# Attention, a dense block and a routed block on one core: three slot tables, and the experts' weights split half an expert ahead

## The chip, the cores and the metric

The kernel runs on one core of one Trainium2 chip. The metric is the device time of one execution in microseconds (us). A core has five engines that run their own instruction queues in order: PE (matrix multiply; its weight loads are listed as PEld), DVE (vector), ACT (scalar), POOL and SP. In this kernel SP issues the plain transfers and POOL the gathers and scatters by index.

## The reference, cut to what matters

```
attn = softmax(mask_64(q k^T / 8)) v               # 4 x 576 tokens = 2304, 8 heads of 64
x    = prelu(attn @ w_in, alpha) @ w_out            # 512 -> 2048 -> 512
logits = x @ w_gate                                 # 8 experts
e    = argmax(logits); p = softmax(logits)[e]
out  = p * (relu(x @ w1[e]) @ w2[e])                # 512 -> 1024 -> 512, only the chosen expert
```

All arrays are float32. The kernel gets that precision by splitting each operand into a high part (rounded to the matmul's format, float32r) and a low part (the rest), and adding three products: high by high, high by low, low by high.

## The kernel before

The 2304 tokens are 18 tiles of 128. They go through attention and the dense block in five blocks of 4, 4, 4, 3 and 3 tiles. `PLAN`, a list of short tokens, gives the order of all work up to the last block. For block j and hidden chunk f (16 of them), `s1` is the first matmul (12 instructions), `act_neg`, `act_sum`, `g_hi`, `g_lo` are the activation and the split, and `s2` the second matmul (9 instructions for 3 tiles).

Behind each block comes the routing of its tokens. `stage_out` copies x out of PSUM; the logits are dot products on DVE (`r_row` loads a row of the gate's weights, `r_dot` multiplies), and for the last block matmuls on PE (`r_trans`, `r_logits`); `r_gate` finds the expert and writes x with its factor to DRAM (`x1d`); `r_rank`, `r_place`, `r_onehot`, `r_list` and `r_add` enter each token into a list by expert.

The experts' stage works in slots: a slot is up to 128 tokens of one expert. `slot_table` says which expert and which piece of its list each slot takes. There are 25 slots, of which the given input uses 21; the first 20 run always, the others under a condition. The first table (6 slots) is made when four blocks are routed and takes full tiles only; the second (19 slots) is made when all are routed and takes the rest.

A slot s runs so: `gather` picks its 128 token numbers on DVE and fetches the rows by a transfer that POOL issues. `xtr` transposes them on PE, copies the high part on ACT and subtracts the low part on DVE. `e1` is the first matmul, in four quarters of 6 instructions; relu on ACT after two of them; `htr` transposes and splits the hidden half; `e2mm` is the second matmul, four quarters of 6; `finish` scales on ACT and scatters. The order on PE is

```
e1 q0, e1 q1, e1 q2, transpose half 0, e1 q3, e2 q0, transpose half 1, e2 q1, transpose x of s+1, e2 q2, e2 q3
```

The expert's weights are 4 MB in four transfers to `raw2[0..3]` (a transfer is skipped if the expert stays the same). They are split in eight pieces, a copy on ACT (`split2_hi`, 128x1024) and a subtraction on DVE (`split2_lo`) each, into 12 ring tiles: the eight of slot s, and four more. A split is made in every slot, whether the expert changes or not. In `slot(s)`, step i splits piece i of slot s+1 and, at each second step, asks for a transfer for slot s+2. The last block is written as a loop with `fill` for what goes between (routing of the fourth block, first table, weights of the first slot), ordered by the framework's scheduler; the slots follow by hand order (`manual_schedule`). The routing of the last block and the second table lie in slots 0 to 3 (`extra`).

Of the kernel before, what the change touches and what calls it, by code (L numbers as in the profile page):

```python
# [19 lines left out]
K1 = 6  # L20
SURE = 20
LO_POOL = ()
# [4 lines left out]
NBT = 4  # L27
PE_MASK = 4
# [52 lines left out]
def attn_moe_moe_kernel(  # L81
# [55 lines left out]
    wgc = const.tile([128, 4, 2 * NE], FP32R, name="wgc")  # L137
# [392 lines left out]
    def r_place(j):  # L530
# [9 lines left out]
        give(("R", j))  # L540
# [19 lines left out]
    def r_onehot(j, h=0):  # L560
        t0, n = BLOCKS[j]
        cf, pf = rc[j]
        ab[j] = []
        for t in range(2 * h, min(2 * h + 2, n)):
# [5 lines left out]
            ab[j].append((t, a, bm))  # L570
# [18 lines left out]
    fill = {}  # L589

    def at(it, prio, fn, *a):
        fill.setdefault(it, []).append((prio, fn, a))

    def run_fill(it):
        for _, fn, a in sorted(fill.pop(it, []), key=lambda e: e[0]):
            fn(*a)

# [3 lines left out]
    def slot_table(part):  # L601
        ns, s0 = (K1, 0) if part == 0 else (NSLOT - K1, K1)

        def small(nm, shape, dt=FP32):
            n = {"cmp": ns * NE, "es": ns, "jn": ns}.get(nm)
            pad = {} if n is None else {"padded_shape": [128, NSLOT] if len(shape) == 1 else [128, NSLOT, NE]}
# [10 lines left out]
        give(("R", NB))  # L617
        yield
# [6 lines left out]
        yield  # L625
# [5 lines left out]
        yield  # L631
# [16 lines left out]
        yield  # L648
# [8 lines left out]
        else:  # L657
            done = small("done", [NE])
# [9 lines left out]
    def table_step():  # L668
        next(gen1, None)
# [381 lines left out]
```

## Time and profile before

| what | value |
|---|---|
| median of 3 runs | 768.34 us (767.71 to 769.11) |
| the profiled execution | 768.02 us |
| its span on the core | 766.2 us |
| PE busy | 747.7 us (98%) |
| DVE busy | 609.1 us (79%) |
| ACT busy | 456.3 us (60%) |
| POOL busy | 89.0 us (12%) |

The last block begins near 415 us, the first slot near 486 us, and the last slot's matmuls end near 758.5 us. A busy time is the time in which an engine had an instruction running; matmuls overlap one another, so PE's busy time hides short waits. The queue before each engine is in order: an instruction that waits holds all behind it.

### The profile page before, as it was taken

How to read it: one execution, taken by the hardware profiler on the slowest of the kernel's cores; microseconds unless marked ns; L12 is line 12 of the kernel's file. 1: busy time of each engine (PE TensorE's matmuls, PEld its weight loads, DVE VectorE, ACT ScalarE, POOL GpSimd, SP SyncE). 2: the span in 40 equal slices, each digit the busy share in tenths (PEclk: the TensorE clock that was granted, in tenths of full speed). 3: DMA queues.
4: the chain of work that ended last, by engine and by line, in shares of the span. 5: the costliest groups of instructions: out<-in, count | busy, mean ns of one | idle time of the engine just before them, and what ended most of it. 6: DMA issues, size and time to landing. Idle time of an engine off the chain costs nothing.

```text
span 766.2 us, 12642 instructions
## 1 busy us (share of the span) xinstructions
PE 747.7 (98%) x4567; PEld 612.6 (80%) x4572; DVE 609.1 (79%) x1154; ACT 456.3 (60%) x868; POOL 89.0 (12%) x106
## 2 busy tenths in 40 slices
PE   7999999999999999999999999999999999999996
PEld 3688888788888888888888988777788888888884
DVE  4999999477556656668775956699999999999997
ACT  4887465533233333334342323778889898899986
POOL 1210001000000000000000001011222213131322
PEclk9999999999999999999999999999999999999998
DMA  9993423233033113122323116430195076766621
GB/s 343 412 367 131 147 74 117 70 86 122 18 100 97 62 57 103 62 97 90 92 69 111 56 42 250 168 119 28 56 340 182 29 270 265 284 236 248 212 75 51
DMA packets 29442, 109.90 MB, mean 143 GB/s; under 512 B 3582, under 2 KB 3966, under 8 KB 22208
## 3 DMA queue, kind: packets, MB, share of 16 engines
q1 hardware_dynamic: 25856, 98.25, 35.6%
q0 software_dynamic: 3520, 10.80, 4.2%
q8 instruction: 38, 0.62, 0.3%
q14 instruction: 28, 0.23, 0.1%
HBM read 154.09 MB, written 10.26 MB: 214 GB/s over the span
## 4 chain that ended last, share of the span: by engine, by line
PE 86%; DVE 8%; issue 2%; DMA 1%; ACT 1%; POOL 0%; SPq 0%; DVEq 0%
PE acc L743 12%; PE h L389 9%; PE acc L431 9%; PE acc L432 9%; PE h L390 8%; PE h L391 8%; PE acc L433 8%; DVE hl L825 4%; PE h L715 4%; PE h L717 4%; PE h L716 4%; PE att L364 2%; PE att L295 2%; PE att L341 2%; PE att L726 1%
## 5 line engine op out<-in xcount | busy, mean ns | idle before, releaser
L825 DVE TENSOR_TENSOR hl<-hl,hl 128x1024 fp32r<-128x1024 f32 x176 | 211.4, 1223 | 17.1 <-ACT hl L819 16.4
L819 ACT CAST hl<-hl 128x1024 fp32r<-128x1024 f32 x176 | 180.2, 1049 | 4.6 <-DMA hl<-in_wx_dram 3.4
L743 PE MATMUL acc<-hl,xl 128*128 128x512 f32 x504 | 130.7, 400 | 2.4 <-DVE xl L730 2.3
L404 ACT ACTIVATE g<-h 128x512 f32<-128x512 f32 (+1 forms) x80 | 44.6, 557 | 142.6 <-PE h L391 112.3
L389 PE MATMUL h<-xh,hl 128*128 128x512 f32 (+1 forms) x320 | 120.5, 377 | 0.7 <-DVE g L408 0.7
L390 PE MATMUL h<-xl,hl 128*128 128x512 f32 (+1 forms) x320 | 118.1, 369 | 0.0
L391 PE MATMUL h<-xh,hl 128*128 128x512 f32 (+1 forms) x320 | 118.0, 369 | 0.0
L432 PE MATMUL acc<-hl,gl 128*128 128x512 f32 x288 | 113.2, 393 | 0.4 <-DVE gl L414 0.4
L433 PE MATMUL acc<-hl,gh 128*128 128x512 f32 x288 | 112.6, 391 | 0.0
L431 PE MATMUL acc<-hl,gh 128*128 128x512 f32 x288 | 109.9, 400 | 0.0
L743 PEld LDWEIGHTS acc<-hl,xl 128*128 128x128 f32 x504 | 91.2, 188 | 21.3 <-DVE xl L730 3.7
L408 DVE SCALAR_TENSOR_TENSOR g<-g,beta,h 128x512 f32<-128x512 f32 (+1 forms) x80 | 55.3, 691 | 56.1 <-ACT g L404 55.9
L414 DVE TENSOR_TENSOR gl<-g,gh 128x512 fp32r<-128x512 f32 (+1 forms) x80 | 50.8, 635 | 38.4 <-PE acc L432 24.1
L349 ACT CAST gh<-g 128x512 fp32r<-128x512 f32 (+1 forms) x80 | 46.5, 581 | 51.4 <-DVE g L408 49.7
L691 POOL DMA_INDIRECT gx<-x1d,ixg x23 | 39.9, 1736 | 290.5 <-DVE xh L703 167.1
L389 PEld LDWEIGHTS h<-xh,hl 128*128 128x128 f32 x320 | 60.1, 188 | 10.9 <-issue 1.2
L715 PE MATMUL h<-hl,xh 128*128 128x512 f32 x168 | 67.7, 403 | 0.0
L485 DVE SCALAR_TENSOR_TENSOR dot<-stage,wge 128x512 bf16<-128x512 f32 x96 | 65.9, 686 | 1.8 <-DMA wge<-in_wgt_dram 0.4
L390 PEld LDWEIGHTS h<-xl,hl 128*128 128x128 f32 x320 | 60.1, 188 | 8.5 <-DVE xl L377 0.5
L717 PE MATMUL h<-hl,xh 128*128 128x512 f32 x168 | 66.1, 393 | 0.3 <-DVE xh L703 0.2
L391 PEld LDWEIGHTS h<-xh,hl 128*128 128x128 f32 x320 | 60.1, 188 | 7.9
L716 PE MATMUL h<-hl,xh 128*128 128x512 f32 x168 | 65.5, 390 | 0.0
(194 smaller groups left out, 1070.8 us busy)
## 6 DMA issues: line engine op xcount, KB each, us to landing
hl<-in_wx_dram SPq DMA_DIRECT2D x92, 1024.0 KB
hl<-in_wcat_dram SPq DMA_DIRECT2D x14, 1024.0 KB
qk<-in_qkv_dram SPq DMA_DIRECT2D x30, 448.0 KB
v<-in_qkv_dram SPq DMA_DIRECT2D x30, 256.0 KB
wge<-in_wgt_dram SPq DMA_DIRECT2D x24, 256.0 KB
x1d<-stage SPq DMA_DIRECT2D x3, 1032.0 KB
hl<-in_qkv_dram SPq DMA_DIRECT2D x6, 448.0 KB
x<-in_wcat_dram SPq DMA_DIRECT2D x2, 1024.0 KB
```

The costliest lines, as they stand in the source:

```text
L389: PE.matmul(out=h[:, 0:n], lhsT=w_in_op(f, k, 0), rhs=xh[:, k, :], start=(k == 0), stop=False)
L390: PE.matmul(out=h[:, 0:n], lhsT=w_in_op(f, k, 0), rhs=xl[:, k, :], start=False, stop=False)
L391: PE.matmul(out=h[:, 0:n], lhsT=w_in_op(f, k, 1), rhs=xh[:, k, :], start=False, stop=(k == 3))
L431: PE.matmul(out=a, lhsT=gh[:, c0:c0 + 128], rhs=w_out_op(f, 0), start=(f == 0), stop=False)
L432: PE.matmul(out=a, lhsT=gl[:, c0:c0 + 128], rhs=w_out_op(f, 0), start=False, stop=False)
L433: PE.matmul(out=a, lhsT=gh[:, c0:c0 + 128], rhs=w_out_op(f, 1), start=False, stop=(f == 15))
L715: PE.matmul(out=o, lhsT=th[:, k, :], rhs=wh, start=(k == 0), stop=False)
L716: PE.matmul(out=o, lhsT=th[:, k, :], rhs=wl, start=False, stop=False)
L717: PE.matmul(out=o, lhsT=tl[:, k, :], rhs=wh, start=False, stop=(k == 3))
L743: PE.matmul(out=o, lhsT=x[:, f % 4, :], rhs=w[:, lo, (f % 2) * 512:(f % 2) * 512 + 512], start=(x is th and f == 0 and lo == 0), stop=(x i ...
L819: ACT.copy(out=t[:, 0, :], in_=r)
L825: eng.tensor_tensor(out=t[:, 1, :], in0=r, in1=f32(t[:, 0, :]), op=ALU.subtract)
```

## The change

`PARTS` makes three tables, of 5, 3 and 17 slots, after three, four and five blocks. The loop of the last block, `fill` and `extra` go; a second list, `PLAN2`, gives the order from the last block's start to the end of slot 8, with one token for each piece of work: `s R t h l u` the dense block (64 to 79 is the last block's f 0 to 15), `N D Z G J j M I i` routing by dot products, `rt ra rl rc` the last block's logits, `y` a step of a table, `v w` the SP register loads and weight transfers, `a d` the two halves of a split (8 for each slot), `g gp` pick and fetch, `Q A f` the three parts of `xtr`, `E k F U z K` a slot's matmul quarters, relu, transposes and their split, `o op` scale and scatter. From slot 9 on, `slot` is the hand order below: it splits pieces 4 to 7 of slot s+1 in its first half and pieces 0 to 3 of slot s+2 in its second. The ring tiles come in the order in which the dense block frees them. The last block's logits are plain float32 matmuls on x as it is, without a split; the split copy of the gate's weights goes, and two float32 filler matmuls near 25 us become four bfloat16 ones. Each transpose takes one of three PSUM banks from a list of free ones.

```diff
-K1 = 6
+PARTS = [(0, 5), (5, 3), (8, 17)]
 SURE = 20
+NPLAN = 9
...
+Q0 g1 R74 J3 a1 u73 t74 gp1 j3 h74 s75 g2 l74 gp2 M6 y3 u74 R75 a3 t75 y4 h75 a5 s76 A0 l75 d1 Q1 R76 u75 A1 t76 w4
...
+w27 F10 E23 gp7 U10 z10 v8 I9 k11 d50 F11 K20 d51 U11 a52 i9 K21 w29 z11 a55 d53 K22 a54 d52 K23 a56 d55 w30 v9 a57
+E24 d56 a59 d54 E25 a58 d57 w31 E26 k12 i8 w32 y8 a60 F12 E27 U12 d58 Q7 z12 k13 A7 d59 F13 K24 U13 d60 a61 w33 K25
+E31 U14 d66 a69 Q8 z14 w37 k15 v11 d68 a71 F15 K28 d69 U15 A8 K29 o6 z15 w38 a70 op6 d71 K30 a72 f8 d70 a73 K31 d72
+a74 w39 E32 a75 d73 E33 a76 d75 w40 E34 k16 d74 a77 F16 d76 w41 a78 E35 d77 U16 k17 z16 a79 w42 F17 g9 K32 d78 o7
+U17 op7 K33 z17 a80 d79 gp9 K34 a81 d80 w43 K35 a82 d81 g10 o8 w44 d82 a83 gp10 d83 op8 w45 Q9 A9 f9
...
     def r_logits(j, t):
-        th, tl = x1t.pop((j, t))
-        n = BLOCKS[j][1]
-        b = rbank(j)
+        x = x1t.pop(t)
+        b = aslot(("rl", t))
+        w = wg.rearrange("p (k e) -> p k e", k=4)
         for k in range(4):
-            PE.matmul(out=b[:, 0:2 * NE], lhsT=th[:, k, :], rhs=wgc[:, k, :], start=(k == 0), stop=False)
-            PE.matmul(out=b[:, 0:NE], lhsT=tl[:, k, :], rhs=wgc[:, k, 0:NE], start=False, stop=(k == 3))
-        lo = rp.tile([128, NE], FP32, tag="lo", name="lo")
-        ACT.copy(out=lo, in_=b[:, NE:2 * NE])
-        DVE.tensor_tensor(out=rt[j][:, t, :], in0=b[:, 0:NE], in1=lo, op=ALU.add)
...
+            PE.matmul(out=b[:, 0:NE], lhsT=x[:, k, :], rhs=w[:, k, :], start=(k == 0), stop=(k == 3))
...
     def ring_tile(s, i):
-        p = 4 + (8 * s + i) % 12
+        p = W_AT[4 + (8 * s + i) % 12]
...
+        toks = [f"E{4 * s}", *both(n, 4), f"E{4 * s + 1}", f"k{2 * s}", *both(n, 5), f"w{4 * s + 10}" if r2 else "",
+                f"E{4 * s + 2}", f"F{2 * s}", f"U{2 * s}", f"z{2 * s}", *both(n, 6), f"E{4 * s + 3}", f"k{2 * s + 1}",
+                *both(n, 7), f"w{4 * s + 11}" if r2 else "", f"K{4 * s}", f"F{2 * s + 1}", f"U{2 * s + 1}",
+                f"z{2 * s + 1}", *both(n + 1, 0)]
+        toks += [f"g{s + 2}", f"gp{s + 2}"] if r2 else []
+        toks += [f"K{4 * s + 1}"] + ([f"Q{n}", f"A{n}", f"f{n}"] if n < NSLOT else []) + both(n + 1, 1)
+        toks += [f"v{s + 3}", f"w{4 * s + 12}"] if r3 else []
+        toks += [f"K{4 * s + 2}", *both(n + 1, 2), f"K{4 * s + 3}", f"o{s}", f"op{s}", *both(n + 1, 3),
+                 f"w{4 * s + 13}" if r3 else ""]
...
-        for s in range(SURE):
+        for o in PLAN2.split():
+            play(o)
+        for s in range(NPLAN, SURE):
             slot(s)
```

How this moves instructions shows in three places. First DVE in slot 4 of before: L825 is a split's subtraction, L730 the low part of a transposed hidden half, L650 to L656 the end of the second table.

```order
L654 TENSOR_TENSOR cmp<-cmp,done 128x152
L655 TENSOR_REDUCE jn<-cmp 128x19
L656 TENSOR_TENSOR col<-col,jn 128x19
L825 TENSOR_TENSOR hl_4809<-hl_4700,hl_4809 128x1024
L825 TENSOR_TENSOR hl_4841<-hl_4700,hl_4841 128x1024
L825 TENSOR_TENSOR hl_4927<-hl_4694,hl_4927 128x1024
L825 TENSOR_TENSOR hl_4933<-hl_4694,hl_4933 128x1024
L730 TENSOR_TENSOR xl<-acc_4983,xl 128x512
```

DVE in slot 4 of the changed kernel: L840 is a split's subtraction, L728 the low part of a hidden half (`xl`) or of x (`xh`), L579 and L581 the last block's one-hot tiles.

```order
L728 TENSOR_TENSOR xl<-att_68,xl 128x512
L840 TENSOR_TENSOR hl_5050<-hl_4511,hl_5050 128x1024
L840 TENSOR_TENSOR hl_5068<-hl_4627,hl_5068 128x1024
L728 TENSOR_TENSOR xl<-att_68,xl 128x512
L840 TENSOR_TENSOR hl_5032<-hl_4627,hl_5032 128x1024
L840 TENSOR_TENSOR hl_4679<-hl_4432,hl_4679 128x1024
L579 TENSOR_SCALAR A<-c,cf 128x152
L581 TENSOR_SCALAR B<-c,pf 128x128
```

Behind a table's steps four splits stood ahead of the hidden half in before; now two stand between one half and the next.

Second, PE at the end of slot 4 of before (L717 the last of `e1` q3, L743 a quarter of `e2`, L726 the transposes of hidden half 1, L699 those of the next slot's x):

```order
L717 MATMUL h<-hl_5063,xh 128x512
L743 MATMUL acc_5067<-hl_4745,xl 128x512 x6
L726 MATMUL att_67<-c,hr 128x128 x4
L743 MATMUL acc_5067<-hl_4777,xl 128x512 x6
L699 MATMUL att_68<-c,gx 128x128 x4
L743 MATMUL acc_5067<-hl_4809,xl 128x512 x6
L743 MATMUL acc_5067<-hl_4841,xl 128x512 x6
L715 MATMUL h<-hl_4927,xh 128x512
```

and PE at the end of slot 8 of the changed kernel, the last of `PLAN2` (L747 the last of `E35`, L717 with `hr` is `F17`, L763 are `K32` to `K35`, L717 with `gx` is `Q9`, then slot 9 begins):

```order
L747 MATMUL h<-hl_5014,xh 128x512
L717 MATMUL acc_4255<-c,hr 128x128 x4
L763 MATMUL acc_5156<-hl_5032,xl 128x512 x6
L763 MATMUL acc_5156<-hl_5068,xl 128x512 x6
L763 MATMUL acc_5156<-hl_5125,xl 128x512 x6
L763 MATMUL acc_5156<-hl_5153,xl 128x512 x6
L717 MATMUL att_67<-c,gx 128x128 x4
L745 MATMUL h<-hl_4679,xh 128x512
```

The transposes of hidden half 1 stand right behind the quarter that makes it, no longer behind a quarter of `e2`; those of slot 9's x stand right ahead of slot 9.

Third, the same place on ACT (L835 `a82`, L768 `o8`, L835 `a83`, L722 `A9`) and on DVE (`g10`, `d82`, `d83`, `f9`) in the changed kernel:

```order
L835 CAST hl_5125<-hl_4511 128x1024
L768 ACTIVATE gx<-acc_5156,gx 128x512
L835 CAST hl_5153<-hl_4511 128x1024
L722 CAST xh<-att_67 128x512
L835 CAST hl_4679<-hl_4627 128x1024
```

```order
L704 CAST ixs<-ixf 128x1
L840 TENSOR_TENSOR hl_5125<-hl_4511,hl_5125 128x1024
L840 TENSOR_TENSOR hl_5153<-hl_4511,hl_5153 128x1024
L728 TENSOR_TENSOR xh<-att_67,xh 128x512
L840 TENSOR_TENSOR hl_4679<-hl_4627,hl_4679 128x1024
```

The low part of slot 9's x (`f9`) stands behind the last split of `PLAN2` (`d83`), whose copy (`a83`) stands behind the scaling of slot 8 (`o8`) and writes the ring tile that `K35` reads.

## Rows read from the trace of the kernel before

**Rows 1.** The page: span, and busy time of each engine.
```profile
span 766.2 us, 12642 instructions
...
PE 747.7 (98%) x4567; PEld 612.6 (80%) x4572; DVE 609.1 (79%) x1154; ACT 456.3 (60%) x868; POOL 89.0 (12%) x106
```

**Rows 2.** Timeline of ACT: scaling of slots 0, 4 and 20 (start, duration).
```profile
506.39 0.69 ACT L749 ACTIVATE gx<-acc,gx 128x512 f32<-128x512 f32 x1 [0.26 <-PE acc L743]
...
561.79 0.69 ACT L749 ACTIVATE gx<-acc,gx 128x512 f32<-128x512 f32 x1 [0.27 <-PE acc L743]
...
758.80 0.69 ACT L749 ACTIVATE gx<-acc,gx 128x512 f32<-128x512 f32 x1 [0.29 <-PE acc L743]
```

**Rows 3.** Busy us by stretch: length, PE, PEld, DVE, ACT, POOL; clock, DMA, GB/s.
```profile
430.00:470.00 40.00, 40.00 (x209) 35.76 (x208) 26.84 (x105) 9.68 (x20) 1.80 (x2) 1.00 0.19 63
470.00:490.00 20.00, 18.93 (x89) 15.31 (x88) 13.80 (x17) 11.16 (x17) 0.32 (x1) 1.00 0.70 290
...
510.00:560.00 50.00, 46.67 (x224) 36.56 (x223) 48.88 (x95) 40.23 (x53) 8.82 (x6) 1.00 0.22 72
...
680.00:700.00 20.00, 20.00 (x99) 16.55 (x98) 19.17 (x26) 17.82 (x24) 5.82 (x4) 1.00 0.51 171
```

**Rows 4.** Timeline of DVE and PE in slot 4.
```profile
550.68 4.67 DVE L825 TENSOR_TENSOR hl<-hl,hl 128x1024 fp32r<-128x1024 f32 x4
...
554.09 1.09 PE L743 MATMUL acc<-hl,xl 128*128 128x512 f32 x4
...
555.27 0.68 DVE L730 TENSOR_TENSOR xl<-acc,xl 128x512 fp32r<-128x512 f32 x1
...
556.00 0.73 PE L743 MATMUL acc<-hl,xl 128*128 128x512 f32 x2 [0.82 <-DVE xl L730]
```

**Rows 5.** Timeline of PE: end of the last block, logits of the last block.
```profile
470.04 0.34 PE L389 MATMUL h<-xh,hl 128*128 128x384 f32 x1
...
472.15 0.86 PE L431 MATMUL acc<-hl,gh 128*128 128x512 f32 x3
...
481.58 0.86 PE L431 MATMUL acc<-hl,gh 128*128 128x512 f32 x3
...
483.66 0.60 PE L699 MATMUL att<-c,gx 128*128 128x128 f32 x4
484.01 0.95 PE L431 MATMUL acc<-hl,gh 128*128 128x512 f32 x3
...
494.89 0.26 PE L463 MATMUL att<-wgc,xh 128*128 128x16 f32 x1
...
495.79 0.47 PE L715 MATMUL h<-hl,xh 128*128 128x512 f32 x1
```

**Rows 6.** Groups by line: instructions, busy us, mean ns of one, idle before.
```profile
L825 DVE TENSOR_TENSOR hl<-hl,hl 128x1024 fp32r<-128x1024 f32 x176 | 211.4, 1223 | 17.1 <-ACT hl L819 16.4
L819 ACT CAST hl<-hl 128x1024 fp32r<-128x1024 f32 x176 | 180.2, 1049 | 4.6 <-DMA hl<-in_wx_dram 3.4 <-PE acc L433 1.2
...
L720 ACT ACTIVATE hr<-h 128x512 f32<-128x512 f32 x42 | 25.2, 600 | 6.3 <-PE h L717 6.2
...
L703 DVE TENSOR_TENSOR xh<-att,xh 128x512 fp32r<-128x512 f32 x22 | 15.0, 681 | 0.0
L749 ACT ACTIVATE gx<-acc,gx 128x512 f32<-128x512 f32 x21 | 14.5, 690 | 5.7 <-PE acc L743 5.7
```

**Rows 7.** Timeline of PE and ACT in slot 20: last matmul of a half, its relu.
```profile
748.75 0.39 PE L717 MATMUL h<-hl,xh 128*128 128x512 f32 x1
...
749.24 0.60 ACT L720 ACTIVATE hr<-h 128x512 f32<-128x512 f32 x1 [0.20 <-PE h L717]
```

**Rows 8.** Timeline of PE near 25 us: the two float32 filler matmuls.
```profile
25.06 1.46 PE L275 MATMUL att<-c 128*128 128x384 f32 x4
```

**Rows 9.** Timeline at the end: the last splits, the last transfer issued.
```profile
759.23 2.50 DVE L825 TENSOR_TENSOR hl<-hl,hl 128x1024 fp32r<-128x1024 f32 x2
...
761.75 0.07 SPq L764 DMA_DIRECT2D hl<-in_wx_dram  x1
```

More of the change, by code (lines that the diff above doesn't have):

```diff
@@ L575, in r_list, with r_add @@
     def r_list(j, h=0):
-        lbs[j] = rbank(j)
-        some = ab.pop(j)
+        lbs[j, h] = aslot(("I", j, h))
+        some = ab.pop((j, h))
         for i, (t, a, bm) in enumerate(some):
-            PE.matmul(out=lbs[j][:, 0:NCOL], lhsT=bm, rhs=a, start=(i == 0), stop=(i == len(some) - 1))
+            PE.matmul(out=lbs[j, h][:, 0:NCOL], lhsT=bm, rhs=a, start=(i == 0), stop=(i == len(some) - 1))
     lbs = {}
-    def r_add(j):
-        DVE.tensor_tensor(out=lst, in0=lst, in1=lbs.pop(j)[:, 0:NCOL], op=ALU.add)
-        give(("R", j))
+    def r_add(j, h):
+        DVE.tensor_tensor(out=lst, in0=lst, in1=lbs.pop((j, h))[:, 0:NCOL], op=ALU.add)
+        give(("I", j, h))
     NB = len(BLOCKS)
[L589 to L596, printed above, removed]
     tab = {}
@@ L657, in slot_table, with table_step @@
         else:
+            tab["scr"] = small("scr", [NCOL])
+        if not final:
             done = small("done", [NE])
             DVE.tensor_tensor(out=done, in0=nb, in1=cum, op=ALU.subtract)
-            DVE.tensor_scalar(out=done, in0=done, scalar1=float(K1), scalar2=0.0, op0=ALU.add, op1=ALU.max)
+            DVE.tensor_scalar(out=done, in0=done, scalar1=float(ns), scalar2=0.0, op0=ALU.add, op1=ALU.max)
             DVE.tensor_tensor(out=done, in0=done, in1=nb, op=ALU.min)
+            if part:
+                DVE.tensor_tensor(out=done, in0=done, in1=tab["done"], op=ALU.add)
             tab["done"] = done
             tab["last"] = ec[:, ns - 1:ns]
-            tab["scr"] = small("scr", [NCOL])
         tab["col", part] = col
         yield
-    def table_step():
-        next(gen1, None)
+    gens = {}
+    def table_step(part):
+        if part not in gens:
+            gens[part] = slot_table(part)
+        next(gens[part])
     def where(s):
-        return (0, s) if s < K1 else (1, s - K1)
+        p = max(i for i, (s0, _) in enumerate(PARTS) if s >= s0)
+        return p, s - PARTS[p][0]
     gat = {}
@@ L679, in attn_moe_moe_kernel, with rows, pick @@
     ops = {}
-    def gather(s):
+    def rows(s):
+        j = NB - len(PARTS) + 1 + where(s)[0]
+        return NT if j == NB else BLOCKS[j][0] * 128
+    def pick(s):
         ixf = rot("ixf", 2, [128, 2], FP32)
@@ L717, in e1, with relu @@
             PE.matmul(out=o, lhsT=tl[:, k, :], rhs=wh, start=False, stop=(k == 3))
-        if kk == 1:
-            hr[s, a] = rot("hr", 2, [128, 512], FP32)
-            ACT.activation(out=hr[s, a], in_=hps.pop((s, a)), func=ACTF.Relu)
-    def htr(s, a):
-        x = hr.pop((s, a))
-        b = pbank("att").rearrange("p (k c) -> p k c", k=4)
-        for k in range(4):
-            PE.transpose(b[:, k, :], x[:, k * 128:k * 128 + 128], ident)
-        th = rot("hth", 2, [128, 4, 128], FP32R)
-        tl = rot("htl", 2, [128, 4, 128], FP32R)
-        ACT.copy(out=th, in_=b)
-        DVE.tensor_tensor(out=tl, in0=b, in1=f32(th), op=ALU.subtract)
-        hT[s, a] = (th, tl)
+    def relu(s, a):
+        hr[s, a] = rot("hr", 2, [128, 512], FP32)
+        ACT.activation(out=hr[s, a], in_=hps.pop((s, a)), func=ACTF.Relu)
     def e2mm(s, ff):
@@ L958, in attn_moe_moe_kernel, with both @@
-    gen1 = slot_table(1)
+    st1.close()
+    e2 = ctx.enter_context(tc.tile_pool(name="e2", bufs=2, reuse_waits="tile"))
+    late = True
+    attb.append(bank("acc3", 1))
+    idle.append(2)
+    def slot(s):
+        def both(n, i):
+            i += 8 * n
+            return [f"a{i}", f"d{i}"] if n < NSLOT else []
+        n = s + 1
+        r2, r3 = s + 2 < NSLOT, s + 3 < NSLOT
+        toks = [f"E{4 * s}", *both(n, 4), f"E{4 * s + 1}", f"k{2 * s}", *both(n, 5), f"w{4 * s + 10}" if r2 else "",
[7 more added lines that the diff above has]
+                 f"w{4 * s + 13}" if r3 else ""]
+        for o in toks:
+            if o:
+                play(o)
```

270 lines of the change are left out of this document (107 added, 163 removed).

## The prediction

> **What bounds the kernel now.** I read the page first: PE is busy 747.7 of a span of 766.2 us, DVE 609.1 and ACT 456.3 [rows 1]. The profiled execution took 768.02 us, 1.8 around its span; the median of the runs shown is 0.32 above it. A gain can thus only come from PE's waits, from fewer PE instructions, or from the ends. Next came the windows of each stretch [rows 3]. The clock granted to PE is 1.00 (the 2.4 GHz level) in all four, so no time is to be had there. In the last block (430 to 470) PE is full and DVE has 26.84 of 40 us: DVE has room. From 470 to 490 PE shows 1.07 us without work, and from 510 to 560, where last routing, second table and splits meet, 3.33 us while DVE is busy 48.88 of 50. In the steady slots (680 to 700) PE is full again and DVE has 19.17 of 20. So PE bounds nearly everything; DVE does between 510 and 560.
>
> The timelines of DVE and PE in slot 4 show how [rows 4]. Four splits in a row (L825) begin at 550.68 and hold DVE until 555.27 or so. Only then comes the low part of the hidden half (L730, 0.68), and PE's next quarter starts at 556.00 with a wait of 0.82 behind it. The four matmuls ahead began at 554.09; at 0.23 each (nine dense ones in 483.66 - 481.58 = 2.08 [rows 5]) PE was free at 555.01, so the gap is 0.99 and the windows understate the waits.
>
> **The steady slot.** ACT scales a slot once at its end; slots 4 and 20 end at 561.79 and 758.80 [rows 2], so a slot of the steady part takes (758.80 - 561.79)/16 = 12.31 us. That is 48 matmuls and 12 transposes back to back; nothing in the change removes one of them.
>
> **Term A, the waits that can go.** I compare the stretch from 470.04 [rows 5] to slot 4's last matmul, 561.79 less its 0.27 of handing over = 561.52 [rows 2], 91.5 us, with the PE work that lies in it. Three pieces of the first dense matmul at 2.11 (470.04 to 472.15), five of the second at 2.08 (481.58 to 483.66), a transposition of four at 0.35 (483.66 to 484.01), three times logits at 0.90 (494.89 to 495.79) and their three transpositions at 0.35 [rows 5], and five slots at 12.31: 6.3 + 10.4 + 0.35 + 2.7 + 1.05 + 61.55 = 82.4. This leaves 9.1 us. Some 13 small matmuls of routing and table remain in either kernel; at 0.11 (an eighth of the logits' 0.90 for a tile's 8 instructions) they are 1.4. So 7.7 us of waits. Bounds: 1.07 + 3.33 = 4.4 below, what the windows show as idle; 9.1 above.
>
> What the change does to them: the first weights are split and slot 0's x is transposed while the last block runs, where DVE has 13 of 40 us free [rows 3], and in slots 0 to 4 no more than two splits stand ahead of a hidden half on DVE (the second order piece), where four stood. A split costs 1.22 on DVE and 1.05 on ACT [rows 6]; two ahead of a low part (0.68) are done in 3.1 us, four in 5.6. A hidden half has about one quarter of six, 1.38 us, plus the transposition as cover, so halving the queue is what matters. With five slots in the first table, made after three blocks and all of one expert for this input, the first slots need the last routing no longer; it spreads over slots 0 to 7. I take all 7.7 as gone.
>
> A check from DVE's side: a steady slot leaves it 0.83 of 20 us, 0.5 in 12.31. Slots 1 to 4 took 561.79 - 506.39 = 55.4 us, at 48.88 of 50 54.2 us of DVE's work; four steady slots hold 47.2. So routing and table cost it some 7 us there, and the splits done half an expert ahead fall into the last block's free time. Eight slots' slack is 4.1 us. What does not fit, up to 6.4 by my count with three more splits (3.5), lies under the new waits of PE below, and I do not add it.
>
> **Term B, new waits.** They are found by walking the new order with durations of before.
>
> At the border of slots 8 and 9 (the second and third order pieces) the transposes `Q9` stand behind `K35`, and slot 9 starts with `f9`'s result. `f9` stands behind `d83`, that behind `a83`, that behind `o8`, which waits for `K35`'s last matmul. `a83` also writes the tile that `K35` reads. The chain is 0.27 handing over [rows 2], 0.69 scaling, 1.05 copy, 1.22 subtraction, 0.68 low part [rows 6] = 3.9 us. PE does its own `Q9` (0.35) and can start the two matmuls of each piece that need the high part only (0.46), 0.8 together: 3.0 us of wait, 2.9 to 3.3. Queued behind are all of slot 9's matmuls, so the whole wait is on the path.
>
> In slots 5 to 8 `F` (the transposition of the second hidden half) stands right behind the quarter `E` that makes it. It waits for the relu: in slot 20 the last matmul began at 748.75 and ended after 0.23, and the relu was over at 749.84 [rows 7], so 0.86 us from one to the other. Between them stand `I9` (0.11), `Q7` or `Q8` (0.35), and nothing for `F17`: 0.75 + 0.5 + 0.5 + 0.86 = 2.6 us. In before a quarter of `e2` (1.38) covered it. Together 5.6 us, 5.0 to 6.2.
>
> From slot 9 on the hand order has `E` q2, `F`, `E` q3, `K`, and the second half's transposes behind a `K`, so the relu is covered. The chain that closes a slot (0.27 + 0.69 + 1.05 + 1.05 + 0.60 = 3.66, scaling, two copies and a relu on ACT [rows 2, 6]) stands against three quarters of the next slot, 4.1. It holds, with some 0.45 to spare, and I cost the loop at nothing.
>
> **Term C, the rest.** The logits become 12 float32 matmuls of 8 columns where 24 of 8 and 16 stood (0.90 a tile). The nearest row is the float32 filler [rows 8]: two instructions of 384 columns, four records, 1.46 us, 0.37 a record, so a float32 instruction has two records. At the small matmul's 0.11 a record 12 instructions are 24 records and 2.7 us, as before; at twice that 5.3, which is 2.6 more. I take nothing, since 8 columns are nearest to the small ones. The split of x that goes saves three subtractions on DVE. The third table adds one small matmul, 0.1, and some 20 small DVE steps that fall in the last block's free time; without that cover they would be some 2 us on DVE. The filler near 25 us stands in time that PE has free and gives nothing.
>
> The rows 8 price per float32 column is 0.73/384 = 1.9 ns an instruction against 0.23/512 = 0.45 for the kernel's usual ones, some four times. The Trainium skill ("FP8 and Floating Point Precision", section "TensorE Precision Notes") says that true FP32 takes four passes through the array. This case's trace agrees for 384 columns; no run shown has 8. By that rule per instruction the logits would be four times 0.11 each, 5.3 in all, and the sum 768.9.
>
> The tail stays as it is. The last splits run to 761.73 and the last transfer is asked for at 761.75 [rows 9], both for slots that the input does not use; the hand order still ends with the same pieces. The gathers are asked for at the same distance, over a slot ahead.
>
> **Sum.** 768.0 - 7.7 + 5.6 + 0.1 = 766.0 against the profiled execution; 766.3 against the median, which is 0.3 above it.
>
> **The rivals.** A measurement of this kernel can tell about 0.2%, 1.5 us, from no change: faster is below 766.8, slower above 769.9.
>
> *Faster by more.* The new waits are smaller than walked: `a83` starts ahead of `K35`'s end, or `F` finds a relu done, and A is at its upper end. 768.3 - 9.1 + 4 = 763.2; with B at nothing and A at 7.7, 760.6. For it: the windows understate waits [rows 3, 4]. Against it: the order at the border is fixed by the rows of three queues.
>
> *No change.* A float32 logits matmul of 8 columns costs twice (+2.6), or DVE stays the bound in slots 0 to 8 and 2.4 of its 6.4 us do not lie under PE's waits: 766.3 + 2.4 = 768.7. For it: 48.88 of 50 on DVE [rows 3], and that the change takes hardly any of DVE's work away. Against it: the free 13 us of 40 in the last block.
>
> *Slower.* In slots 9 to 20 the copies of a split wait for PE's reading of the tile that they overwrite, half an expert ahead, so ACT and DVE have no lead. The chain of 3.66 has 0.45 to spare; if its steps come 0.75 later (one scaling's turn on ACT), each of twelve slots grows by 0.3 and the result is 766.3 + 3.6 = 769.9; from there it is slower, and at 0.4 a slot it is 771.1. For it: DVE has only 0.5 us a slot free, ACT 2.2 of 20 [rows 3], and copies waited for PE 1.2 us in before [rows 6]. Against it: the walk through three loop slots came out steady.
>
> That the change does nothing at all I exclude, since 4.4 us of waits are shown to lie where the order is rewritten.
>
> **How the numbers follow.** The forecast holds 0.50, with a range of its own of 764.4 (A 8.5 and B 4.5) to 768.0 (A at 6). Faster by more 0.17, no change 0.20, slower 0.13. Most of the forecast (0.42) is below 766.8, the rest is within; with the second case, 0.59 faster. Same: 0.08 + 0.18 = 0.26. Slower: 0.13 + 0.02 of the third case = 0.15. The range leaves out a tenth on either side: 761.5 to 770.0.
>
> **What the profile after would show.** Right, if PE from 470 to slot 4's end has under 1 us without work and slot 4's scaling comes near 554; if slot 9's first quarter has a stop of about 3 us behind `f9`, and four transpositions of slots 5 to 8 stop 0.5 to 0.9 each behind a relu; if slots 9 to 20 come every 12.3 us; and if three logits take 0.9 each. Wrong, if PE has many waits on DVE in slots 0 to 4, if a loop slot is over 12.5, or if logits take 1.8 each.

## The result, and the profile after

The changed kernel takes 778.31 us (median of 4 runs, 776.34 to 782.63) where before takes 768.11: ratio 1.0138, 95% interval 1.0091 to 1.0186. It is slower by some 10 us; 2 us less were forecast. The profiled execution took 782.63 us, and the rows below are its own. It is the longest of the four, 4.3 above their median, so the sizes read from it are those of a long execution; why the four differ by 6 us stays open.

The page after, against [rows 1]: PE is busy 4.6 us more in a span that is 14.7 longer.

```profile
span 780.9 us, 12749 instructions
...
PE 752.3 (96%) x4568; PEld 616.7 (79%) x4573; DVE 617.1 (79%) x1177; ACT 459.6 (59%) x869; POOL 90.5 (12%) x106
```

Windows of the changed kernel, columns as in [rows 3]:

```profile
430.00:470.00 40.00, 39.19 (x205) 34.77 (x205) 30.80 (x106) 13.53 (x24) 3.31 (x3) 1.00 0.51 172
470.00:490.00 20.00, 20.00 (x102) 17.92 (x101) 18.54 (x46) 10.93 (x19) 0.00 (x0) 1.00 0.05 14
510.00:560.00 50.00, 45.93 (x244) 38.36 (x243) 41.77 (x78) 37.21 (x50) 8.97 (x6) 0.97 0.49 174
560.00:600.00 40.00, 38.26 (x183) 30.86 (x182) 38.02 (x62) 32.38 (x42) 5.89 (x4) 1.00 0.65 233
600.00:640.00 40.00, 33.63 (x143) 26.45 (x142) 31.19 (x42) 28.80 (x36) 9.50 (x7) 0.91 0.59 205
680.00:700.00 20.00, 19.81 (x97) 16.06 (x97) 18.52 (x27) 17.45 (x23) 5.47 (x3) 1.00 0.47 187
```

PE's waits of 470 to 490 are gone. It now stands still in the last block (430 to 470), near 550, and above all from 600 to 640, with DMA busy 0.49 of the time from 510 to 560, where before had 0.22, and the granted clock at 0.91 from 600 to 640. Busy transfer queues alone don't stop PE: before moves as much in the next two stretches, and its PE is full there.

```profile
560.00:600.00 40.00, 40.00 (x195) 33.13 (x194) 38.17 (x53) 36.17 (x46) 10.59 (x7) 1.00 0.59 221
600.00:640.00 40.00, 40.00 (x198) 33.09 (x197) 37.80 (x49) 36.17 (x46) 9.80 (x8) 1.00 0.62 221
```

Scaling of slots 0, 4 and 20 (ACT) in the changed kernel, against [rows 2]:

```profile
502.33 0.69 ACT L768 ACTIVATE gx<-acc,gx 128x512 f32<-128x512 f32 x1 [0.44 <-PE acc L763]
...
564.12 0.69 ACT L768 ACTIVATE gx<-acc,gx 128x512 f32<-128x512 f32 x1
...
772.82 0.69 ACT L768 ACTIVATE gx<-acc,gx 128x512 f32<-128x512 f32 x1 [0.29 <-PE acc L763]
```

Slot 0 is scaled 4.1 us earlier than before, slot 4 2.3 later, slot 20 14.0 later. Slots 0 and 20 are scaled right behind their last matmul, but `o4` stands in `PLAN2` behind the first two quarters of slot 5: slot 4's last matmul starts at 562.17, where before had 561.36, only 0.8 later. To see where the time goes, I add up over PE's matmuls the time from one start to the next less the median of that kind. A slot's row ends where its last matmul (`K`) starts. The first two columns explain the difference: 24.4 - 9.9 = 14.5, and the two profiled executions differ by 782.63 - 768.02 = 14.6.

| lost on PE, us | before | changed | eight index tiles (x1) | no transfers (x2) | order repaired (x5) | best (x8) | x5 without transfers (x10) |
|---|---|---|---|---|---|---|---|
| last block, 415 to 470 | 1.1 | 3.9 | 3.7 | 3.8 | 3.9 | 2.7 | 3.6 |
| 470 to the end of slot 3 | 6.9 | 0.7 | 0.9 | 0.8 | 0.6 | 0.7 | 0.6 |
| slot 4 | 1.7 | 5.8 | 0.4 | 0.6 | 0.3 | 0.3 | 0.3 |
| slots 5 to 8 | 0.1 | 8.6 | 8.0 | 3.0 | 5.8 | 2.4 | 3.9 |
| slot 9, with its border to slot 8 | 0.0 | 4.6 | 4.6 | 4.7 | 1.2 | 2.3 | 1.2 |
| slots 10 to 20 | 0.2 | 0.8 | 1.9 | 0.7 | 0.2 | 0.9 | 1.0 |
| sum, before rounding | 9.9 | 24.4 | 19.5 | 13.7 | 12.1 | 9.4 | 10.5 |

**Near 550.** Timelines of POOL, DVE and PE:

```profile
545.29 3.23 POOL L772 DMA_INDIRECT out_dram<-gx,ixs  x1 [6.45 <-ACT gx L768]
...
549.69 0.15 DVE L703 TENSOR_SCALAR ixg<-ixf 128x1 int32<-128x1 f32 x1
553.96 0.15 DVE L704 CAST ixs<-ixf 128x1 int32<-128x1 f32 x1 [4.12 <-DMA out_dram<-gx,ixs]
554.03 0.68 DVE L728 TENSOR_TENSOR xl<-att,xl 128x512 fp32r<-128x512 f32 x1
...
550.21 0.61 PE L717 MATMUL acc<-c,gx 128*128 128x128 f32 x4
554.86 0.96 PE L717 MATMUL att<-c,hr 128*128 128x128 f32 x4 [4.04 <-DVE xl L728]
```

`g7` writes the index tile that the scatter of slot 3 reads (four tiles in turn). The scatter is asked for at 545.29 and lands at 553.96, 8.7 us later, with weights of slots 5 and 6 on the queues; the low part behind `g7` waits, and PE behind that.

**560 to 612.** Asks on SP, timelines of ACT and PE:

```profile
597.48 0.33 SPq L790 DMA_DIRECT2D hl<-in_wx_dram  x1
...
602.31 0.33 SPq L790 DMA_DIRECT2D hl<-in_wx_dram  x1
...
605.21 1.05 ACT L835 CAST hl<-hl 128x1024 fp32r<-128x1024 f32 x1 [0.46 <-DMA hl<-in_wx_dram]
606.16 0.59 ACT L751 ACTIVATE hr<-h 128x512 f32<-128x512 f32 x1
606.65 1.04 ACT L835 CAST hl<-hl 128x1024 fp32r<-128x1024 f32 x1
609.78 1.04 ACT L835 CAST hl<-hl 128x1024 fp32r<-128x1024 f32 x1 [2.10 <-DMA hl<-in_wx_dram]
610.73 0.58 ACT L722 CAST xl<-att 128x512 fp32r<-128x512 f32 x1
611.21 0.60 ACT L751 ACTIVATE hr<-h 128x512 f32<-128x512 f32 x1
...
606.80 0.66 PE L717 MATMUL att<-c,hr 128*128 128x128 f32 x4 [0.96 <-ACT hr L751]
...
611.87 0.66 PE L717 MATMUL acc<-c,hr 128*128 128x128 f32 x4 [3.01 <-ACT hr L751]
```

PE's row blames the relu (L751). The relu stands in ACT's queue behind copies (L835) of slot 9's weights, and these wait for transfers (`w38`, `w39`) that land 7.7 and 7.5 us behind their ask. From the rows of SP and ACT, ask and first copy of the four tiles of two slots in a row with new experts:

| | asked | copied |
|---|---|---|
| before, slots 6 and 7 | 555.4 558.3 562.3 564.7, 567.4 570.6 574.6 577.0 | 7.7 to 8.5 later each, no copy waits |
| changed, slots 8 and 9 | 578.6 583.9 586.7 590.2, 592.3 594.6 597.5 602.3 | 7.6 5.0 4.9 7.0, 8.3 8.1 7.7 7.5 later; those of 590.2, 597.5 and 602.3 wait |

The trace also has the moment of each transfer's last semaphore update. For the four tiles of the second slot of the pair it comes 6.7 to 7.8 us behind the ask in before and 7.4 to 8.0 in the changed kernel: the transfers take about as long in either. What `PLAN2` has less of is the time between an ask and its copy. Nor could these asks come earlier in this order of splits: each of the eight comes at most 0.13 us behind the end of the subtraction that reads the tile's old content last.

**The border of slots 8 and 9**, and the clock behind a stop (windows, granted clock in the third column from the end):

```profile
619.63 0.69 ACT L768 ACTIVATE gx<-acc,gx 128x512 f32<-128x512 f32 x1 [0.31 <-PE acc L763]
620.22 1.03 ACT L835 CAST hl<-hl 128x1024 fp32r<-128x1024 f32 x1
621.15 0.59 ACT L722 CAST xh<-att 128x512 fp32r<-128x512 f32 x1
...
621.79 0.50 PE L745 MATMUL h<-hl,xh 128*128 128x512 f32 x1 [1.76 <-ACT xh L722]
622.13 0.40 PE L746 MATMUL h<-hl,xh 128*128 128x512 f32 x1
623.16 0.72 PE L747 MATMUL h<-hl,xh 128*128 128x512 f32 x1 [0.64 <-DVE xh L728]
```

```profile
556.00:558.00 2.00, 2.00 (x6) 1.56 (x5) 2.00 (x3) 0.93 (x2) 0.00 (x0) 0.50 0.55 98
612.00:616.00 4.00, 4.00 (x14) 3.24 (x15) 3.83 (x9) 2.85 (x4) 2.08 (x2) 0.63 0.17 66
...
624.00:627.00 3.00, 3.00 (x9) 2.28 (x9) 0.72 (x1) 1.04 (x1) 0.00 (x0) 0.55 0.99 352
```

**The last block.** One row of the gate lands late behind the first weights, and two list matmuls that had others between them now stand one apart:

```profile
452.40 0.69 DVE L497 SCALAR_TENSOR_TENSOR dt<-stage,wg 128x512 bf16<-128x512 f32 x1 [3.17 <-DMA wg<-in_wgt_dram]
...
419.60 0.80 PE L591 MATMUL att<-A,B 128*128 128x152 f32 x2 [0.59 <-DVE B L581]
```

The first cost PE 1.0 us (454.2), the second 1.5 in three pieces.

### The profile page after: what moved, and what is told of

Read it like the earlier page. It is cut to its first block, busy times and chain, and to the rows that moved or that the text cites. A ratio compares the mean times of both kernels' runs of the same rounds, so it can differ in the third digit from the quotient of the medians.

```text
span 780.9 us, 12749 instructions
## 1 busy us (share of the span) xinstructions
PE 752.3 (96%) x4568; PEld 616.7 (79%) x4573; DVE 617.1 (79%) x1177; ACT 459.6 (59%) x869; POOL 90.5 (12%) x106
## 5 line engine op out<-in xcount | busy, mean ns | idle before, releaser
L840 DVE TENSOR_TENSOR hl<-hl,hl 128x1024 fp32r<-128x1024 f32 x180 | 214.5, 1220 | 15.5 <-ACT hl L835 14.8
L835 ACT CAST hl<-hl 128x1024 fp32r<-128x1024 f32 x180 | 183.5, 1049 | 16.0 <-DMA hl<-in_wx_dram 6.3
L763 PE MATMUL acc<-hl,xl 128*128 128x512 f32 x504 | 130.8, 405 | 0.4 <-ACT xl L722 0.4
L446 PE MATMUL acc<-hl,gh 128*128 128x512 f32 x288 | 115.4, 401 | 0.0
L448 PE MATMUL acc<-hl,gh 128*128 128x512 f32 x288 | 112.7, 391 | 0.0
L763 PEld LDWEIGHTS acc<-hl,xl 128*128 128x128 f32 x504 | 93.9, 193 | 19.5 <-ACT xl L722 0.9
L429 DVE TENSOR_TENSOR gl<-g,gh 128x512 fp32r<-128x512 f32 (+1 forms) x80 | 50.7, 634 | 27.6 <-ACT gh L364 14.7
L747 PE MATMUL h<-hl,xh 128*128 128x512 f32 x168 | 66.6, 396 | 0.8 <-DVE xh L728 0.8
L446 PEld LDWEIGHTS acc<-hl,gh 128*128 128x128 f32 x288 | 54.1, 188 | 12.0 <-issue 1.0
```

Of the source, the lines that this page charges most:

```text
L446: PE.matmul(out=a, lhsT=gh[:, c0:c0 + 128], rhs=w_out_op(f, 0), start=(f == 0), stop=False)
L448: PE.matmul(out=a, lhsT=gh[:, c0:c0 + 128], rhs=w_out_op(f, 1), start=False, stop=(f == 15))
L747: PE.matmul(out=o, lhsT=tl[:, k, :], rhs=wh, start=False, stop=(k == 3))
L763: PE.matmul(out=o, lhsT=x[:, f % 4, :], rhs=w[:, lo, (f % 2) * 512:(f % 2) * 512 + 512], start=(x is th and f == 0 and lo == 0), stop=(x i ...
L835: ACT.copy(out=t[:, 0, :], in_=r)
L840: DVE.tensor_tensor(out=t[:, 1, :], in0=r, in1=f32(t[:, 0, :]), op=ALU.subtract)
```

## The experiments

Theories: **1** the reuse of the index tile, **2** the weight transfers, **3** the order as predicted (relu and border), **4** DVE's backlog. All ratios are to before.

**x1: eight index tiles.**

```diff
-        ixs = rot("ixs", 4, [128, 1], I32)
+        ixs = rot("ixs", 8, [128, 1], I32)
```

> The changed kernel with eight scatter index tiles in place of four (the profile of the changed kernel shows DVE 4.12 us behind the scatter of slot 3 at 549.69, PE 4.04 behind DVE and some 2 us at half clock after it). Theory 1, the reuse of the index tile stops DVE: the stop near 550 goes with its slow matmuls (5.8 us of excess in that stretch), time near 772.5. Theory 2, the weight transfers set the end of slots 5 to 9: the stop near 550 goes, but the stops that wait for weights behind it grow by as much, time 777 to 778. Theory 3, the order alone (relu and border waits as predicted) costs the time: no change of the stop, 778.

Measured: 776.61, ratio 1.011 (1.0088 to 1.0132). The stop is gone (slot 4 loses 0.4 in place of 5.8), but the median is only 1.7 less, and the intervals of x1 and of the changed kernel overlap. So the medians don't settle how much of the stop comes back. The traces point to theory 2: ACT waits 3.33 for weights where it waited 2.30 in the changed kernel. And x9 below, which still has the stop, took 776.14 in its profiled execution where x1 took 776.69; its slots 5 to 8 lose 4.4 us, those of x1 8.0. x1's timeline of DVE and ACT:

```profile
549.88 0.14 DVE L704 CAST ixs<-ixf 128x1 int32<-128x1 f32 x1
...
592.94 1.04 ACT L835 CAST hl<-hl 128x1024 fp32r<-128x1024 f32 x1 [3.33 <-DMA hl<-in_wx_dram]
```

**x2: no transfers for slots 5 to 9.**

```diff
         e, ch = regs[s]
+        if 5 <= s <= 9:
+            return
```

> The changed kernel with no weight transfer for slots 5 to 9 (these slots compute with the weights that are there, so expert 0's tokens get the wrong expert). Theory 2, the transfers of 16 MB for four changes of expert in five slots: the scatter of slot 3 lands in some 4 to 6 us instead of 8.7, the stop near 550 falls under 1.5 us, and the stops behind weight copies (0.6, 1.1 and 3.2 us) fall to the relu handoff alone (under 0.9): 768 to 770. Theory 1: the scatter still takes its own 4 us of landing, so a stop of 1 to 4 us stays near 550: 772 to 775. Theory 3: stops stay, 777 to 778.

Measured: 771.14, 1.0034 (1.0022 to 1.0045). 7.2 us of the 10.2 go with the transfers, a little less than theory 2 said (768 to 770); in the table they go from slot 4 (5.8 to 0.6) and slots 5 to 8 (8.6 to 3.0). The scatter now lands after 5.0 us (545.16 to 550.16), the wait is 0.45. What is left is the last block and theory 3: the relu's stops in the sizes predicted, and the border, which still costs 4.7. Timelines of DVE and PE in x2:

```profile
550.16 0.15 DVE L704 CAST ixs<-ixf 128x1 int32<-128x1 f32 x1 [0.45 <-DMA out_dram<-gx,ixs]
...
563.99 0.33 PE L717 MATMUL acc<-c,hr 128*128 128x128 f32 x1 [0.68 <-ACT hr L751]
...
602.30 0.66 PE L717 MATMUL acc<-c,hr 128*128 128x128 f32 x4 [0.75 <-ACT hr L751]
...
610.04 0.66 PE L717 MATMUL att<-c,gx 128*128 128x128 f32 x4 [1.60 <-DMA gx<-x1d,ixg]
611.37 0.54 PE L745 MATMUL h<-hl,xh 128*128 128x512 f32 x1 [0.67 <-ACT xh L722]
```

The four relu stops are 0.80, 0.47, 0.47 and 0.92 from start to start. At the border another wait shows that was hidden: `gp9` is asked for so late that the fetched rows land 1.60 behind PE.

**x3: the border repaired** (fetch of slot 9 a slot earlier, its transposes behind `K33`).

```diff
-... K31 d72 ... K33 z17 a80 d79 gp9 K34 ... op8 w45 Q9 A9 f9
+... K31 g9 gp9 d72 ... K33 z17 Q9 A9 f9 a80 d79 K34 ... op8 w45
```

> The changed kernel with pick and fetch of slot 9 moved ahead by a slot and the transposes of slot 9's x with their split behind the second quarter of slot 8's e2, as in the loop. Theory 3, the border wait is the chain scaling, copy, subtraction, low part: the 4.6 us of excess behind the border go down to under 0.5, time near 774. Theory 2: the wait at the border is for weights of slot 9 or 10; the stop stays or moves into slot 9, 777 to 778.

**x4: the second half's transposes a quarter later.**

```diff
-F11 K20 ... F13 K24 ... F15 K28 ... F17 g9 K32
+K20 F11 ... K24 F13 ... K28 F15 ... g9 K32 F17
```

> The changed kernel with the transposes of the second hidden half of slots 5 to 8 one quarter of e2 later. Theory 3, the relu handoff is uncovered: four stops of 0.48 to 0.9 go and the one of 3.2 falls to 1.8, so 2.5 to 3.5 us less, 775 to 776. Theory 2: PE runs out at the copies that wait for weights, whatever stands ahead: the same time, 777.5 to 778.5, with the stops moved by a quarter.

Measured: x3 776.77, 1.0114 (1.0074 to 1.0154); x4 778.97, 1.0151 (1.0128 to 1.0174). In x3 the border's stop is gone (slot 9 loses 1.2 in place of 4.6), of which 1.5 reaches the median, between what the two theories said. x4 wins nothing in the median, as theory 2 expects: slots 5 to 8 still lose 5.3, in fewer and longer stops (2.9 in one, behind a relu that stands behind a copy). As for x1, both intervals overlap the changed kernel's.

**x5: the three together.** The edits of x1, x3 and x4.

> The three repairs of the order together: eight index tiles, slot 9's fetch and transposes earlier, second hidden halves one quarter later. If the waits add up (theories 1 and 3), the stop at 550 (5.5 us with its slow matmuls), the border (4.2) and the relu handoffs (2.7) all go: 766. If the weight transfers set the end of slots 5 to 9 (theory 2), what each gave alone is the measure (1.7, 1.5 and nothing), the rest turns into waits for weights: 774 to 776.

Measured: 772.37, 1.0049 (1.0034 to 1.0065), 5.9 less than the changed kernel where the three alone gave 1.7, 1.5 and -0.7. Neither theory had this (766, or 774 to 776). It looks as if each stop covers for another, and taking one away pays only when the next is gone too; but the three single differences are within the changed kernel's own spread, so this is likely and not shown.

**x6, x7: two changes of expert less.** The second table's slots in descending order of experts; x6 in the changed kernel, x7 in x5.

```diff
+        if part == 1:
+            order = small("order", [ns])
+            DVE.tensor_scalar(out=order, in0=siota[:, 0:ns], scalar1=-1.0, scalar2=float(ns - 1), op0=ALU.mult, op1=ALU.add)
```

> The changed kernel with the second table's three slots in descending order of experts (one more small DVE instruction), the output being the same: slots 0 to 6 then have one expert, changes come at slots 7 and 9 and no longer at 5, 6, 8 and 9, 8 MB less to move. Theory 2 (transfers): close to the run without transfers, 771.1, so 771 to 773. Theory 1 (index tile): the stop near 550 goes only if the scatter lands earlier, and the rest stays: 775 or more. Theory 3 (order): 778.

> The three repairs of the order and the second table in descending order. Theory 2 with the order's own waits (from the run without transfers, 771.1: relu handoffs 2.7 and border 4.2 with its slow matmuls, 0.5 near 550): 763.7, and up to 766 if two of the four changes still cost something. If the transfers of slots 7 and 9 bind as those of 8 and 9 did: 769 to 772.

Measured: x6 773.79, 1.0054 (1.0033 to 1.0075); x7 771.39, 1.003 (1.002 to 1.0039). x6 supports theory 2 with all the weights that the slots need: 8 MB less are 4.5 us, a little short of its 771 to 773. x7 misses 763.7 by 7.7 and lies where two changes of expert that still bind were put (769 to 772): of slot 9's four transfers, asked for from 587 on, the last two are still late for their copies.

**x8: x7, copies behind relus, one weight tile behind the gate's rows.** **x16: those copies in x5 alone.**

```diff
-... E33 a76 d75 w40 E34 k16 d74 a77 F16 d76 w41 a78 E35 d77 U16 k17 z16 a79
+... E33 d75 w40 E34 k16 d74 F16 w41 E35 U16 k17 z16 a76 d76 a77 d77 w42 K32 F17 o7 U17 a78
-... l69 w3 D109 ... N31 u70
+... l69 D109 ... N31 w3 u70
```

> As the run before it, and two things more: the fourth tile of slot 0's weights is asked for behind the last row of the gate (in the last block a row landed 3.2 us late behind the weights and PE stopped 1.05), and five copies of weights on ACT stand behind the relus and hidden halves that are ready before them. If row and weights meet as read: 1.0 less than the run before; if the copies that wait hold up the relus (0.5 to 2.1 us each in the changed kernel) up to 3 less where transfers still bind, nothing where they no longer do. So 1 to 4 less than the run before it; the rival, that a copy behind the relu comes too late for its own matmul: the same or up to 2 more.

> The kernel with the three repairs of the order (772.4, all four changes of expert) with five copies of weights on ACT behind the relus and hidden halves that are ready before them. If the late weights reach PE through the copies that stand ahead of the relus on ACT: the stops of 0.9, 1.1 and 1.6 us between 592 and 605 go, 769 to 770. If the weights themselves are what PE waits for: 772 to 773.

Measured: x8 767.72, 0.9987 (0.9977 to 0.9998), 3.7 less than x7: before's time, 0.1% under it; x16 770.19, 1.002 (1.0012 to 1.0029), 2.2 less than x5. So by the medians a good part of the price of late weights is the order on ACT: a copy that waits holds a relu that is ready. Traces show it for x8, whose slots 5 to 8 lose 2.4 where x7's lose 6.6. The profiled executions of x5 and x16 took the same time (770.54 and 770.58): in x16 the stops of 0.92 and 1.58 behind ACT are gone, and others have come.

**x9, x11: one subtraction in eight left out** in slots 2 to 9, in the changed kernel and in x8.

```diff
+        if 2 <= s <= 9 and i == 3:
+            return
         DVE.tensor_tensor(out=t[:, 1, :], in0=r, in1=f32(t[:, 0, :]), op=ALU.subtract)
```

> The changed kernel without one of the eight subtractions on DVE in slots 2 to 9 (piece 3; its low part keeps old numbers, so these slots lose precision): 8 x 1.22 = 9.8 us less work on DVE. Theory 2 in its plain form (16 MB through the transfer queues in five slots): the time stays at 777 to 779. Theory 4 (DVE's backlog from the last routing frees the weight tiles late, so transfers are asked for late and the next copies wait): the stops behind copies at 598 to 609 (0.6, 1.1, 3.2) fall to the relu handoff alone, the one at 550 and the border stay: 772 to 775.

> The best kernel so far (order repaired, second table descending, row and copies moved: 767.7) without one of eight subtractions in slots 2 to 9 (9.8 us less on DVE, less precision). Theory 4: the stops of 1.6 us before 600 and 2.1 behind it go: 763.5 to 765. Theory 2: the two transfers of experts still bind: 767 to 768.

Measured: x9 778.56, 1.0137 (1.0112 to 1.0161); x11 767.1, 0.9986 (0.9974 to 0.9998). Eight subtractions less, 9.8 us by their mean of 1.22 (DVE's busy time falls by 8.4 and 8.6), change nothing: as the cause of these kernels' time theory 4 falls.

**x10: x5 without transfers.** The edits of x5 and x2.

> The three repairs of the order together (772.4) and no weight transfer for slots 5 to 9 (wrong expert for some slots). Theory 2: what is left of stops behind 560 goes, only the 3.9 us of the last block and crumbs stay: 763 to 765. Theory 4: without transfers the copies no longer wait, but DVE is still 97 to 99% busy from 540 on and its backlog meets PE directly: 767 to 770.

Measured: 768.25, 1.000 (0.9989 to 1.001). Theory 2 alone expected 763 to 765; the number is that of theory 4. x9 and x11 exclude theory 4 where transfers are under way, but no run took work from DVE in x10. Its trace is for theory 4 there: DVE is busy 79.2 of the 82 us from 540 to 622, and in slots 5 to 9 PE loses 3.2 us in three stops behind it, 1.27 where the low part stands behind the last steps of the third table and a split (below), 0.88 and 1.05 where it stands behind three splits in a row. x10's timelines of DVE and PE:

```profile
574.04 0.18 DVE L659 TENSOR_TENSOR col<-col,jn 128x17 f32<-128x17 f32 x1
574.14 1.22 DVE L842 TENSOR_TENSOR hl<-hl,hl 128x1024 fp32r<-128x1024 f32 x1
575.27 0.68 DVE L728 TENSOR_TENSOR xl<-att,xl 128x512 fp32r<-128x512 f32 x1
...
576.01 0.74 PE L763 MATMUL acc<-hl,xl 128*128 128x512 f32 x2 [1.10 <-DVE xl L728]
```

**x12: x8 with one subtraction of eight on POOL** (slots 3 to 9, piece 5).

```diff
+        eng = POOL if 3 <= s <= 9 and i == 5 else DVE
+        eng.tensor_tensor(out=t[:, 1, :], in0=r, in1=f32(t[:, 0, :]), op=ALU.subtract)
```

> As the best kernel so far (767.7), with the subtraction of piece 5 in slots 3 to 9 on POOL in place of DVE (same output; 7 x 1.22 = 8.5 us less on DVE; no run shows how long POOL takes for it, it has 50 of 60 us free). Theory 4, if POOL takes under some 6 us: 764 to 766. If POOL is slower, or its fetches are held up behind it, or DVE slows beside it: 768 to 772.

Measured: 770.71, 1.0031 (1.002 to 1.0043), 3 more than x8; the reason stands at the end.

**x13, x14: the last block's stops**, in the changed kernel (with x8's move of `w3`) and in x8.

```diff
-... M5 l63 I5 i5 N24 s64 N25
+... M5 l63 N24 s64 I5 i5 N25
```

> The changed kernel with the second list matmuls of the third block (and their sum) behind the first dense matmul of the last block, and the fourth tile of slot 0's weights asked for behind the last gate row. If the last block's stops are a loss of their own: 2.6 less, 775 to 776. If weights set the time behind 560 anyway (theory 2): what is won there comes back as waits, 777.5 to 778.5.

> The repaired kernel with two changes of expert less (767.7) and the list matmuls moved in the same way. Own loss: 1.5 less, 766.2. Theory 2: 767.5 to 768.

Measured: x13 778.28, 1.014 (1.0114 to 1.0166); x14 767.78, 0.9993 (0.9984 to 1.0003). The edit did not do its work: in the trace the two list matmuls now stand one behind the other with nothing between, and stop PE for 1.4 us. Only the gate's row is repaired in x13 (3.9 to 3.1 lost), and nothing of that shows in the time.

**x15: half the bytes of each transfer of slots 5 to 9.**

```diff
+        h = 1024 if 5 <= s <= 9 else 2048
-        SP.dma_start(out=raw2[t], ...
+        SP.dma_start(out=raw2[t][:, 0:h], ...
```

> The changed kernel with half of each weight transfer of slots 5 to 9 left out (512 KB in place of 1 MB, the other half keeps what was there, so these slots compute with mixed weights). Theory 2a, the queue of bytes: near the run without transfers (771.1), 771 to 774, and the stop near 550 under 2 us. Theory 2b, a delay of each transfer that its size does not set: 777 to 779.

Measured: 774.56, 1.0072 (1.0059 to 1.0085): 3.75 of the 7.2 us with half the bytes, the number of asks unchanged. The price goes with the bytes in the queue (2a), a little above its range, and the stop near 550 is 2.2; 2b falls.

## Why the prediction was wrong

**Term A was right in size.** From 470 to the end of slot 4 before loses 6.9 + 1.7 = 8.6, the changed kernel without transfers 0.8 + 0.6 (x2): 7.2 gone, where 7.7 was taken. With the transfers a new stop, that of the index tile, takes back 5.2 of it in slot 4. And the cover that was named for the moved work, DVE's free time in the last block, hides DVE's work and not the transfers: the gate's rows now queue behind the first weights, and with the list matmuls the last block loses 2.7 more (3.8 in x2, 1.1 in before).

**Term B was right for the relus** (2.66 in x2, 2.6 taken) and short at the border, which costs 4.6 us in place of 3.0 (by its own addends 3.1). In the changed kernel's profile the chain is the one walked: 3.8 us from the end of slot 8's last matmul to the first one that reads `f9`'s result, 3.9 by the walk, of which PE stands still for 2.7. But the matmuls behind it run at half clock for a while, which is the rest. In the seven other traces with the border as it was, the first stop there is another, that for slot 9's rows (1.1 to 1.9).

**Term C was right.** A tile's float32 logits take 0.81 (timeline of PE, eight records):

```profile
510.40 0.96 PE L477 MATMUL att<-c,rx 128*128 128x8 f32 x8
511.21 0.48 PE L763 MATMUL acc<-hl,xl 128*128 128x512 f32 x1
```

**What failed is a step that wasn't made: the transfers were not costed.** They stand in none of the three terms, so the sum has them at nothing, without a reason. Three tables bring two pairs of new experts, slots 5 and 6 and slots 8 and 9, 16 MB in five slots. Before has such a pair as well (its slots 6 and 7), but copies 7.7 to 8.5 us behind each ask, when the weights are there. In `PLAN2` the copies of slots 8 and 9 start 4.9 to 8.3 us behind, with the waits for weights in it, and every wait for weights stands on ACT ahead of a relu. 7.2 of the 10.2 us go with the transfers (x2), half of that with half the bytes (x15). The sentence "The gathers are asked for at the same distance, over a slot ahead" was wrong for slot 9, whose `gp9` is asked for 4.5 us ahead of its transposes (614.90, 619.43), and it left out the tile that a pick overwrites: `g7` comes 4.4 us behind the scatter that still reads it.

**The rivals.** "Slower" put 769.9 and more down to copies in the loop. That side came true, but not by its mechanism: but for one slot of 12.79, slots 10 to 20 take 12.30 to 12.32 each, and the time was lost ahead of them. DVE, on which a rival and a check were built, does not bound the changed kernel (x9). But the check's words that what does not fit on DVE lies under PE's new waits bear out in x10: with those waits and the transfers gone, PE stops behind DVE instead (and in the last block), and the time is that of before, not the 761 that the sum without term B would give.

From forecast to time: 766.3 + 7.2 (transfers) + 2.7 (last block) + 1.6 (border) = 777.8, against 778.3. The first figure is a difference of medians, the other two are read from traces, and the terms overlap, as x10 shows: the sum is a tally and not a proof. Open stays how much an earlier ask alone would give, since the tiles are not free earlier, and what the list matmuls cost.

## What to carry to other kernels

Where an order is rewritten, list for each transfer the ask, the bytes ahead of it and the first reader, for old and new order, before any engine is costed; then look at what stands behind that reader in its queue. A tile that is used in turn ties a step to whatever read it last, and a step that is moved ahead is moved towards that reader. And measure repairs of stops together as well: here one alone gave 1.7, 1.5 or nothing, each within the kernel's own spread of 6, and three gave 5.9.

## What the runs showed of the hardware

Behind the stops of 4.04 and 3.01 us, and at the border behind 1.76 and 0.64 with two matmuls between, PE was granted the lower of its two levels for some us (0.50 from 556 to 558, 0.63 and 0.55 in the other two windows above): start-to-start times of a 512-column matmul were 0.43 in place of 0.23. That cost 1.2 to 1.8 us each time, on top of the stop. In x8, whose longest stop behind 470 is 1.2, the granted clock stays at 1.00 to the last slot.

The scatter of slot 3, 128 rows, landed 5.0 us behind its ask with no weights under way (x2), 6.6 with half of them (x15) and 8.7 with all.

POOL held up DVE in x12. Timelines of DVE in the changed kernel, and of DVE, POOL and PE in x12:

```profile
566.33 0.23 DVE L627 TENSOR_TENSOR t<-c,nb 128x64 f32<-128x64 f32 x1
```

```profile
560.53 2.77 DVE L627 TENSOR_TENSOR t<-c,nb 128x64 f32<-128x64 f32 x1
...
560.80 2.40 POOL L845 TENSOR_TENSOR hl<-hl,hl 128x1024 fp32r<-128x1024 f32 x1
...
565.49 0.72 PE L767 MATMUL acc<-hl,xl 128*128 128x512 f32 x1 [2.51 <-DVE xl L732]
```

A step of 0.23 us took 2.77 while POOL subtracted, and ended 0.1 us behind it; PE then waited 2.51. Splits of DVE beside POOL's took up to 2.82 in place of 1.22, while steps that read one operand from PSUM kept their 0.7. In all DVE is busy 617.9 us in x12 and 617.1 in x8: what was taken from it came back as steps held up. The Trainium skill ("SBUF — State Buffer", section "SBUF: two separate sides") says that the two engines share a port pair that is locked for a whole instruction; x12 agrees, in that DVE's step ended with POOL's instruction, though by the rows it began 0.27 us ahead of it.
